# Attention and two fused feed-forward layers on one core: four buffers for raw weight blocks, and a later change of PSUM pools

## The chip, the cores and the metric

The kernel runs on one core of a Trainium2 chip. The metric is device time in microseconds (us) of one launch, as the median of several. A core has a tensor engine (PE, whose weight loads are shown apart as PEld), a vector engine (DVE), a scalar engine (ACT), a general engine (POOL) and a queue for transfers (SP, from which all the transfers named here are issued). PSUM has eight banks; a tile of 128 x 512 f32 fills one.

## The reference

All is f32; in short (softmax, mu and var written as words). The attention result, put back to 2304 tokens of 512, goes through two feed-forward blocks:

```python
scores = scale * np.matmul(q, k.transpose(0, 1, 3, 2))       # 4 x 8 heads, S = 576, D = 64
cum = np.cumsum(np.maximum(s, 0.0), axis=-1)
bias = -(cum[:, :, :, None] - cum[:, :, None, :])
scores = np.where(causal, -1000000000.0, scores + np.minimum(bias, 0.0))
attn = softmax(scores); x = attn @ v
...
a = x @ w1; b = x @ w2                                        # 512 -> 1024
y = (a * b @ w3) @ w_out                                      # 1024 -> 1024 -> 512
...
h = y @ w_in                                                  # 512 -> 1024
solu = h * softmax(h)
ln = (solu - mu) / np.sqrt(var + 1e-06) * g_ln
out = ln @ w_out2                                             # 1024 -> 512
```

## The kernel before, in words

Large products are made of three products of shorter words: each operand is split into a high and a low word by `hi` (a copy with rounding, on ACT) and `lo` (a subtraction, L100, on DVE or POOL), and PE multiplies high by high, high by low and low by high. The Tile framework turns the program into one fixed order of instructions per engine; at run time an engine takes its list from the top and waits at an instruction until the semaphores that it names have come.

**Phase one, the attention (to about 393 us).** A loop of 36 steps. A step does the scores of one head (`sc`; L170 for the first eight heads, L178 and L179 later), its softmax (L192 and L196), and of an earlier head the transposes (`tr`) and the product with V (`av`). Between them lie units of the first feed-forward block: `ab_unit` does 12 matmuls into a tile `a` (L326), which ACT evicts to `a_sb` (L338), and 12 into `b`, which DVE multiplies by `a_sb` into `g_sb` (L346). After the last step 16 such units of the last batch stand alone. For later heads the low words of Q and K (tile QK, L100) are made by POOL.

**Raw weight blocks.** The weights lie in HBM as 64-bit numbers. `stage` (L407) loads a block of 128 x 512 of them, 512 KB, into a buffer named `stage`; `to_f32` turns it into f32 with one pass on ACT (L363) and three on DVE (L369, L370, L374); then `hi` and `lo` make its words, or the f32 block is spilled for later. `load_jobs` keeps as many loads ahead as `stg[1]` says, which is also the number of buffers; in the attention the pool `at` holds two. `pump(n)` converts n blocks; the table PUMP does that in steps 3, 5, 6, 10 to 16 and 22 to 33. After the attention `stg` is set to another pool and four buffers (`mp`), before and after the change.

**Between the phases: M.** M = w3 @ w_out is made in eight blocks f = 0 to 7 by `m_unit`: 24 matmuls of 128 x 512 each (L637), from the words of w3 (`w3h`, `w3l`, eight converted half blocks kept ahead) and of w_out (`WOH`, `WOL`). ACT evicts a block's high word to `MH`, DVE its low word to `ML` (L100). In the same stretch DVE and ACT convert the remaining w3 blocks and make words of spilled weights (`wf_words`: IT..., IB...) and of the first g tile (`split_g`). I call a block's matmuls m0 to m7.

**Phase two.** Per 256 tokens: x = M applied to g (L721, `x2_half`), then h by a seven-product scheme (L753), softmax and layer norm, and the output (L847, `out_unit`). Its PSUM tiles come from psC (four fixed ones) and psD (four turning buffers).

**PSUM pools.** The attention uses psA and psB and from step 11 psE and psF (two fixed banks, six turning). `smalltile` takes the next buffer of the second pool. Where a pool is closed and another opened over its banks, a first write to a bank waits for the last reader of what stood in that bank.

Of the kernel before, what the change touches and what calls it, by code (L numbers as in the profile page):

```python
# [15 lines left out]
PSUM = bass.MemoryType.PSUM  # L16
# [10 lines left out]
def tile_attention_moe(  # L27
# [29 lines left out]
    for i in range(4, 0, -1):  # L57
# [7 lines left out]
    ps_ctx = ExitStack()  # L65
    PSP = [
        ps_ctx.enter_context(tc.tile_pool(name="psA", bufs=2, space=PSUM)),
        ps_ctx.enter_context(tc.tile_pool(name="psB", bufs=4, space=PSUM)),
    ]
# [17 lines left out]
    def smalltile(name):  # L87
        return PSP[1].tile([128, 512], F32, tag="B", name=name)
# [4 lines left out]
    def hi(dst, src, eng=None):  # L93
        if eng is None:
            nc.scalar.activation(out=dst, in_=src, func=AF.Copy)  # L95
        else:
            eng.tensor_copy(out=dst, in_=src)

    def lo(dst, src, hi_, eng=nc.vector):
        eng.tensor_tensor(out=dst, in0=src, in1=hi_.bitcast(F32), op=ALU.subtract)  # L100
# [3 lines left out]
    at = attn_ctx.enter_context(tc.tile_pool(name="at", bufs=1, side="left"))  # L104
# [288 lines left out]
    jobs = []  # L393
    loaded = []

    stg = [at, 2]

    def stage(src):
        raw = stg[0].tile([128, CW, 2], U32, tag="stage", bufs=stg[1], name="stage")
# [15 lines left out]
    def pump(n):  # L415
        for _ in range(n):
            load_jobs()
            if loaded:
                raw, conv = loaded.pop(0)

                with ExitStack() as order:
                    for ins in behind:
                        order.enter_context(tc.issue_after(ins))
                    conv(raw)
        load_jobs()
# [206 lines left out]
    def m_unit(f):  # L632
        ps = smalltile("m")
        for k in range(KF):
            H3, L3 = m_st[f, k // 4]
            for w_, o_ in ((H3, WOH), (H3, WOL), (L3, WOH)):
                nc.tensor.matmul(  # L637
                    ps, w_[:, k % 4], o_[:, k],
                    start=(k == 0 and w_ is H3 and o_ is WOH), stop=(k == KF - 1 and w_ is L3),
                )  # L640
        hi(MH[:, f], ps)
        lo(ML[:, f], ps, MH[:, f])
# [8 lines left out]
    for i in range(8):  # L651
# [7 lines left out]
            nm[0] += 1  # L659
    behind.clear()  # L660
    right0.close()
    ps_ctx.close()
    PSP[:] = [
        ctx.enter_context(tc.tile_pool(name="psC", bufs=1, space=PSUM)),
        ctx.enter_context(tc.tile_pool(name="psD", bufs=4, space=PSUM)),
    ]
    HD = DF // 2

    r2 = ctx.enter_context(tc.tile_pool(name="r2", bufs=1, side="right"))
# [13 lines left out]
    def load_g(c):  # L683
        t0 = c * 256
        g_hl[c] = [None] * KP
        for p in range(KP):
            g_hl[c][p] = [None, r2.tile([128, 2, 256], F32R, tag=f"gl{p}", bufs=2, name=f"gl{p}")]
        for p2_ in range(0, KP, 2):
            done = 0
            while done < 256:  # L690
                n, o = divmod(t0 + done, S)
                w = min(256 - done, S - o)
                for p in (p2_, p2_ + 1):
                    nc.sync.dma_start(
                        out=g_hl[c][p][1][:, :, done:done + w].bitcast(F32),
                        in_=g_scr[n][2 * p:2 * p + 2, :, o:o + w].rearrange("f p t -> p f t"),
                    )
                done += w

    def split_g(c):  # L700
        for p in range(KP):
            raw = g_hl[c][p][1]
            g_hl[c][p][0] = r2.tile([128, 2, 256], F32R, tag=f"gh{p}", bufs=1, name=f"gh{p}")
            hi(g_hl[c][p][0], raw.bitcast(F32))
            lo(raw, raw.bitcast(F32), g_hl[c][p][0], V)
# [190 lines left out]
    def wf_words(i):  # L896
        t = wf.pop(i)
        if i < 14:
            n, j = WN[WL[i]][:-1], int(WN[WL[i]][-1])
            h_, l_ = (x[:, j] for x in IT[n])  # L900
        else:
            h_, l_ = OH[:, i - 14], OL[:, i - 14]
        hi(h_, t)
        lo(l_, t, h_, V)
        wf_load(i + 5)
# [3 lines left out]
        wf_load(i)  # L909
    load_g(1)  # L910
    for f in range(nm[0], KF):
        m_unit(f)
        pump(AM[f])
        if f < 6:
            wf_words(f)
        if f == 5:
            split_g(0)
# [101 lines left out]
```

## Time and profile before

| | |
|---|---|
| three timed runs | 739.62, 737.88, 738.95 us; median 738.95 |
| profiled execution | 737.73 us; span from first to last instruction 736.0 us |
| mean granted PE clock | 0.997 of full speed |
| PE busy | 716.7 us, 97% |
| DVE busy | 504.9 us, 69% |
| ACT busy | 468.0 us, 64% |
| blocks loaded by `stage` | 48 (32 of them counted under `in_w_dram`, 16 under `in_wo_dram`) |

The span is one execution; 1.73 us of its time lie outside the span. Busy shares are means over stages with different limits. Times in rows are from the start of the span.

### The profile page before, as it was taken

What the parts mean: (1) busy time and instruction counts of PE and PEld (TensorE: products, weight loads), DVE (VectorE), ACT (ScalarE), POOL (GpSimd) and SP (SyncE); (2) the same over time, 40 slices, a digit from 0 to 9 for tenths busy, and PEclk for the clock granted to TensorE, in tenths of its full rate; (3) what the DMA queues carried; (4) which work ended last, traced back from release to release, by engine and by line L of the source; (5) the groups of instructions that cost most, each with busy time, mean ns of one, the idle gap of its engine ahead of it and who ended that gap; (6) DMA issues with size and microseconds to landing.
All of it is one profiled execution on the core that took longest, in us unless ns stands there. A gap on an engine that the chain in (4) does not pass through costs nothing.

```text
span 736.0 us, 13040 instructions
## 1 busy us (share of the span) xinstructions
PE 716.7 (97%) x4682; PEld 625.0 (85%) x4682; DVE 504.9 (69%) x1267; ACT 468.0 (64%) x985; POOL 99.5 (14%) x102
## 2 busy tenths in 40 slices
PE   9889998999999999999998999999999999999997
PEld 6567978888888899899997889988888988888886
DVE  7987978897678888632887876576747365563651
ACT  4987777898766777732544745577646465564652
POOL 5033313142221331000000000001000000000000
PEclk9999999999999999999999999999999999999999
DMA  4644554655476665614566943253234142304221
GB/s 109 186 126 99 174 161 142 194 144 130 127 221 186 182 188 149 208 61 147 170 215 202 355 149 101 58 110 75 79 82 101 44 123 75 89 12 75 44 57 44
DMA packets 79829, 95.52 MB, mean 130 GB/s; under 512 B 41418, under 2 KB 52682, under 8 KB 79764
## 3 DMA queue, kind: packets, MB, share of 16 engines
q1 hardware_dynamic: 79764, 94.69, 45.0%
q8 instruction: 37, 0.61, 0.3%
q14 instruction: 28, 0.23, 0.1%
HBM read 59.04 MB, written 20.14 MB: 108 GB/s over the span
## 4 chain that ended last, share of the span: by engine, by line
PE 73%; DVE 11%; DMA 8%; ACT 5%; issue 2%; POOL 1%; SPq 0%; ACTq 0%; DVEq 0%; POOLq 0%
PE x L721 14%; PE o L847 13%; PE b L326 10%; PE a L326 10%; PE hX L753 5%; DMA stage<-in_w_dram 5%; PE av L298 4%; PE hZ L753 3%; PE tr L265 3%; ACT P L196 2%; PE sc L170 2%; PE sc L178 2%; DVE P L192 2%; DVE stage L374 2%; PE hW L753 2%
## 5 line engine op out<-in xcount | busy, mean ns | idle before, releaser
L196 ACT ACTIVATE P<-P,STAT 128x576 f32<-128x576 f32 (+4 forms) x160 | 88.3, 554 | 31.5 <-DVE STAT L192 30.9
L100 POOL TENSOR_TENSOR QK<-qk,QK 64x1152 fp32r<-64x1152 f32 x24 | 67.1, 2798 | 167.2 <-ACT QK L95 158.9
L721 PE MATMUL x<-gl,MH 128*128 128x256 f32 x288 | 80.4, 280 | 0.0
L721 PE MATMUL x<-gh,ML 128*128 128x256 f32 x288 | 80.2, 279 | 0.0
L721 PE MATMUL x<-gh,MH 128*128 128x256 f32 x288 | 79.9, 280 | 0.0
L192 DVE CUSTOM_DVE_ANT_0 P<-sc,wmask 128x576 f32<-128x576 f32 (+4 forms) x160 | 70.6, 478 | 4.5 <-PE sc L170 3.2
L326 PE MATMUL a<-xT0h,W 128*128 128x288 f32 x256 | 58.1, 300 | 1.9 <-ACT a_sb L338 1.9
L326 PE MATMUL b<-xT0h,W 128*128 128x288 f32 x256 | 57.6, 299 | 1.5 <-DVE STAT L192 0.8
L847 PE MATMUL o<-OH,lh 128*128 128x512 f32 x144 | 57.1, 397 | 0.2 <-DVE ll L100 0.2
L326 PE MATMUL a<-xT1h,W 128*128 128x288 f32 x256 | 57.2, 298 | 0.0
L847 PE MATMUL o<-OH,ll 128*128 128x512 f32 x144 | 57.0, 396 | 0.0
L847 PE MATMUL o<-OL,lh 128*128 128x512 f32 x144 | 57.0, 396 | 0.0
L326 PE MATMUL b<-xT1h,W 128*128 128x288 f32 x256 | 56.5, 295 | 0.0
L721 PEld LDWEIGHTS x<-gl,MH 128*128 128x128 f32 x288 | 54.2, 188 | 1.3
L817 DVE COPY lt<-turned 128x2048 uint16<-128x2048 uint16 x16 | 21.9, 1368 | 48.4 <-DMA turned<-half 48.4
L721 PEld LDWEIGHTS x<-gh,MH 128*128 128x128 f32 x288 | 54.0, 188 | 1.1
L721 PEld LDWEIGHTS x<-gh,ML 128*128 128x128 f32 x288 | 54.1, 188 | 0.9
L346 DVE TENSOR_TENSOR g_sb<-b,a_sb 128x288 f32<-128x288 f32 x64 | 28.8, 449 | 32.8 <-PE b L326 16.7
L363 ACT ACTIVATE stage<-stage 128x512 f32<-128x512 f32 x56 | 36.9, 674 | 21.2 <-DMA stage<-in_w_dram 18.0
L298 PE MATMUL av<-PT,VT 128*64 128x64 f32 (+4 forms) x384 | 50.1, 395 | 0.0
L231 ACT ACTIVATE P<-P,STAT 128x576 f32<-128x576 f32 x64 | 42.7, 717 | 10.4 <-DVE STAT L226 10.4
L338 ACT ACTIVATE a_sb<-a 128x288 f32<-128x288 f32 x64 | 25.6, 401 | 33.3 <-PE a L326 33.1
(193 smaller groups left out, 1965.5 us busy)
## 6 DMA issues: line engine op xcount, KB each, us to landing
stage<-in_w_dram SPq DMA_DIRECT2D x32, 512.0 KB
g_scr<-g_sb SPq DMA_DIRECT2D x32, 288.0 KB
stage<-in_wo_dram SPq DMA_DIRECT2D x16, 512.0 KB
qk<-in_qk_dram SPq DMA_DIRECT2D x24, 288.0 KB
QK<-QK SPq DMA_DIRECT2D x24, 288.0 KB
gl<-g_scr SPq DMA_DIRECT2D x24, 256.0 KB
wf<-wf_scr SPq DMA_DIRECT2D x22, 256.0 KB
out_dram<-o SPq DMA_DIRECT2D x18, 256.0 KB
```

The lines of the kernel that those rows point to most:

```text
L100: eng.tensor_tensor(out=dst, in0=src, in1=hi_.bitcast(F32), op=ALU.subtract)
L192: mx = nc.vector.tensor_tensor_reduce(out=dst2, in0=ps_in, in1=msk, scale=-SCALE, scalar=BIG, op0=ALU.add, op1=ALU.min, accum_out=st[0:row ...
L196: ex = nc.scalar.activation(out=dst, in_=dst, func=AF.Exp, bias=st[0:rows, ti:ti + 1], scale=-1.0, accum_out=st[0:rows, 5 + ti:6 + ti],)
L231: nc.scalar.activation(out=dst, in_=dst, func=AF.Copy, scale=r)
L298: nc.tensor.matmul(st["ps"][64 * e:64 * e + 64, 448 + c0:448 + c1], vr[:, j, e], PT[(2 * p + e) % 4][:, o + c0:o + c1], **kw,)
L326: nc.tensor.matmul(ps, w_[:, c, fs], x_[:, c, sl], start=(c == 0 and w_ is WH and x_ is XH), stop=(c == KC - 1 and w_ is WL),)
L338: ab_last[0] = nc.scalar.activation(out=a_sb, in_=ps, func=AF.Copy).ins
L346: ab_last[1] = nc.vector.tensor_tensor(out=g[:, sl], in0=ps, in1=st["a"], op=ALU.mult).ins
L363: nc.scalar.activation(out=high.bitcast(F32), in_=high.bitcast(F32), func=AF.Copy, scale=2.0 ** -112)
L721: last = nc.tensor.matmul(ps[:, a], w_[:, k, m * 128:m * 128 + 128], g_[:, k % 2], start=(k == 0 and w_ is MH and g_ is GH), stop=(k == KF ...
L753: last_h[0] = nc.tensor.matmul(ps, x_[:, k], w_[:, k], start=first and k == 0 and x_ is XH and w_ is WH, stop=k == 1 and x_ is XL, skip_gr ...
L847: nc.tensor.matmul(ps, l_[:, k], w_[:, k], start=(k == 0 and l_ is LH and w_ is OH), stop=(k == KF - 1 and l_ is LL),)
```

## The change

`stage` gets four buffers in the attention, and up to four loads are ahead there. The closing of the attention's pools and the opening of psC and psD move from the end of the attention to the loop over the blocks of M, ahead of block 6: m0 to m5 take tiles of psF, m6 and m7 and everything later tiles of psD.

```diff
--- before.py
+++ after.py
@@ -393,7 +393,7 @@
     jobs = []
     loaded = []
 
-    stg = [at, 2]
+    stg = [at, 4]
 
     def stage(src):
         raw = stg[0].tile([128, CW, 2], U32, tag="stage", bufs=stg[1], name="stage")
@@ -659,11 +659,6 @@
             nm[0] += 1
     behind.clear()
     right0.close()
-    ps_ctx.close()
-    PSP[:] = [
-        ctx.enter_context(tc.tile_pool(name="psC", bufs=1, space=PSUM)),
-        ctx.enter_context(tc.tile_pool(name="psD", bufs=4, space=PSUM)),
-    ]
     HD = DF // 2
 
     r2 = ctx.enter_context(tc.tile_pool(name="r2", bufs=1, side="right"))
@@ -909,6 +904,12 @@
         wf_load(i)
     load_g(1)
     for f in range(nm[0], KF):
+        if f == 6:
+            ps_ctx.close()
+            PSP[:] = [
+                ctx.enter_context(tc.tile_pool(name="psC", bufs=1, space=PSUM)),
+                ctx.enter_context(tc.tile_pool(name="psD", bufs=4, space=PSUM)),
+            ]
         m_unit(f)
         pump(AM[f])
         if f < 6:
```

What the order of instructions shows at three places. Numbers in names count allocated tiles, so the same thing may have another number after the change.

PE, the first block of M. `b_4852` is the last b tile of the attention, `m_4936` (`m_4928` after) is m0. Before:

```order
L326 MATMUL b_4852<-xT1l_132,W12_127 128x288
L326 MATMUL b_4852<-xT1h_131,W13_128 128x288
L637 MATMUL m_4936<-WOH_4263,w3h_4637 128x512 [waits DMAHW3_49,DMAHW4_49,DMAHW2_49,DMAHW6_49,DMAHW1_49,DMAHW7_49,DMAHW0_49,DVE_49]
L637 MATMUL m_4936<-WOL_4264,w3h_4637 128x512
L637 MATMUL m_4936<-WOH_4263,w3l_4638 128x512
```

After:

```order
L326 MATMUL b_4852<-xT1l_132,W12_127 128x288
L326 MATMUL b_4852<-xT1h_131,W13_128 128x288
L637 MATMUL m_4928<-WOH_4263,w3h_4637 128x512 [waits DMAHW5_49,DMAHW4_49,DMAHW6_49,DMAHW3_49,DMAHW7_49,DMAHW0_49,Activation_49]
L637 MATMUL m_4928<-WOL_4264,w3h_4637 128x512
L637 MATMUL m_4928<-WOH_4263,w3l_4638 128x512
```

m0 no longer names a semaphore of DVE; before, that was the last read of `b_4852` (L346), and now there is one of ACT, an eviction of an earlier a tile.

PE, the end of m5 and the start of m6. `m_5183` (`m_5175` after) is m5, `m_5226` is m6. Before:

```order
L637 MATMUL m_5183<-WOL_4264,w3h_5075 128x512
L637 MATMUL m_5183<-WOH_4263,w3l_5076 128x512
L637 MATMUL m_5226<-WOH_4263,w3h_5116 128x512 [waits Activation_49]
L637 MATMUL m_5226<-WOL_4264,w3h_5116 128x512
L637 MATMUL m_5226<-WOH_4263,w3l_5117 128x512 [waits DVE_49]
```

After:

```order
L637 MATMUL m_5175<-WOL_4264,w3h_5067 128x512
L637 MATMUL m_5175<-WOH_4263,w3l_5068 128x512
L637 MATMUL m_5226<-WOH_4263,w3h_5108 128x512 [waits DVE_49]
L637 MATMUL m_5226<-WOL_4264,w3h_5108 128x512
L637 MATMUL m_5226<-WOH_4263,w3l_5109 128x512
```

The first matmul of m6 waited for the words of w3 on ACT; it now waits for DVE, by the count the low word ML of m5, which stands in the same bank as m6 does now.

PE, further on in m6. `m_5253` is m7, `x2_5286` the first tile of phase two. Before:

```order
L637 MATMUL m_5226<-WOH_4263,w3h_5124 128x512 [waits Activation_49]
L637 MATMUL m_5226<-WOL_4264,w3h_5124 128x512
L637 MATMUL m_5253<-WOH_4263,w3h_5163 128x512 [waits Activation_49]
L637 MATMUL m_5253<-WOL_4264,w3h_5163 128x512
L721 MATMUL x2_5286<-gh0_5214,MH_4258 128x256 [waits DMAHW4_49,DMAHW3_49,DMAHW5_49,DMAHW2_49,DMAHW6_49,DMAHW1_49,DMAHW7_49,DMAHW0_49,DVE_49]
L721 MATMUL x2_5286<-gl0_4910,MH_4258 128x256
L721 MATMUL x2_5286<-gh0_5214,ML_4259 128x256
```

After:

```order
L637 MATMUL m_5226<-WOH_4263,w3h_5116 128x512 [waits Activation_49]
L637 MATMUL m_5226<-WOL_4264,w3h_5116 128x512
L637 MATMUL m_5253<-WOH_4263,w3h_5155 128x512 [waits Activation_49]
L637 MATMUL m_5253<-WOL_4264,w3h_5155 128x512
L716 MATMUL x2_5286<-gh0_5206,MH_4258 128x256 [waits DMAHW4_49,DMAHW5_49,DMAHW3_49,DMAHW6_49,DMAHW2_49,DMAHW7_49,DMAHW1_49,DMAHW0_49]
L716 MATMUL x2_5286<-gl0_4902,MH_4258 128x256
L716 MATMUL x2_5286<-gh0_5206,ML_4259 128x256
L637 MATMUL m_5226<-WOH_4263,w3l_5117 128x512 [waits DVE_49]
```

Before, 20 matmuls of x stand here before m6 goes on; now three, and 12 more matmuls of m6 and m7 come earlier than those of x. Up to here m6 has done 12 matmuls in both.

DVE, around the low word of m2 (`m_5038` before, `m_5030` after); the L369 with `stage_4971` (`stage_4963`) is the first pass of a raw w3 block that waits for its load. Before:

```order
L100 TENSOR_TENSOR IB21l_4892<-wf_4926,IB21h_4891 128x512 [waits DMAHW4_49,Activation_49]
L100 TENSOR_TENSOR w3l_5025<-stage_4875,w3h_5024 128x512 [waits PE_49,Activation_49]
L369 TENSOR_SCALAR stage_4971<-stage_4971 128x512 [waits DMAHW1_49]
L370 SCALAR_TENSOR_TENSOR stage_4971<-stage_4971 128x512 [waits DVE_49,Activation_49]
L100 TENSOR_TENSOR ML_4259<-m_5038,MH_4258 128x512 [waits Activation_49]
```

After:

```order
L100 TENSOR_TENSOR IB21l_4884<-wf_4918,IB21h_4883 128x512 [waits DMAHW4_49,Activation_49]
L100 TENSOR_TENSOR w3l_5017<-stage_4875,w3h_5016 128x512 [waits PE_49,Activation_49]
L100 TENSOR_TENSOR ML_4259<-m_5030,MH_4258 128x512 [waits Activation_49]
L369 TENSOR_SCALAR stage_4963<-stage_4963 128x512 [waits DMAHW1_49]
L370 SCALAR_TENSOR_TENSOR stage_4963<-stage_4963 128x512 [waits DVE_49,Activation_49]
```

ML of m2 now stands ahead of the two passes of that block. Between this place and ML of m5 both orders hold the same passes but for this one.

## Rows read from the trace of the kernel before

**Rows 1.** The page's busy time by engine, over the whole span.

```profile
PE 716.7 (97%) x4682; PEld 625.0 (85%) x4682; DVE 504.9 (69%) x1267; ACT 468.0 (64%) x985; POOL 99.5 (14%) x102
```

**Rows 2.** Busy time, clock, DMA share and GB/s in three windows of the attention.

```profile
73.00:160.00 87.00, 81.71 (x623) 73.28 (x622) 76.02 (x221) 70.90 (x177) 23.28 (x8) 1.00 0.56 166
160.00:300.00 140.00, 140.00 (x1104) 125.52 (x1102) 108.67 (x323) 107.07 (x272) 35.87 (x13) 1.00 0.60 171
300.00:320.00 20.00, 18.80 (x149) 18.24 (x146) 12.95 (x40) 12.41 (x30) 0.00 (x0) 1.00 0.46 150
```

**Rows 3.** Waits from 73 to 160 us: total, times, longest.

```profile
DVE stage L369 <- DMA stage<-in_w_dram: 10.0, 8, 3.1
...
ACT stage L363 <- DMA stage<-in_w_dram: 4.1, 3, 2.8
```

**Rows 4.** The chain from 73 to 165 us, by line.

```profile
by line: DMA stage<-in_w_dram 23.6%; DVE P L192 11.3%; DVE W L100 10.5%; DVE stage L374 7.2%; DVE stage L370 6.1%; DVE P L233 5.8%; PE b L326 5.7%; PE a L326 5.5%; DVE PT L97 4.7%; issue 3.6%; ACT P L196 2.0%; PE tr L265 1.9%; PE sc L178 1.
```

**Rows 5.** Timeline of ACT: four evictions of an a block.

```profile
74.55 0.41 ACT L338 ACTIVATE a_sb<-a 128x288 f32<-128x288 f32 x1 [0.60 <-PE a L326]
...
160.01 0.39 ACT L338 ACTIVATE a_sb<-a 128x288 f32<-128x288 f32 x1
...
198.80 0.39 ACT L338 ACTIVATE a_sb<-a 128x288 f32<-128x288 f32 x1
...
220.90 0.39 ACT L338 ACTIVATE a_sb<-a 128x288 f32<-128x288 f32 x1
```

**Rows 6.** The chain from 296 to 322 us: start, length, what.

```profile
303.68 6.18 DMA stage<-in_wo_dram
...
309.93 0.68 ACT stage L363
...
314.54 1.58 PE a L326 x12
```

**Rows 7.** Lo passes of tile W (ns minimum/median/maximum); two spans, POOL and DVE.

```profile
L100 DVE TENSOR_TENSOR W<-stage,W x16: 643/677/2461, 29.0 to 155.0; 128x512 fp32r<-128x512 f32 x16
...
82.74 5.76 POOL L100 TENSOR_TENSOR QK<-qk,QK 64x1152 fp32r<-64x1152 f32 x2 [13.42 <-ACT QK L95]
...
86.59 2.46 DVE L100 TENSOR_TENSOR W<-stage,W 128x512 fp32r<-128x512 f32 x1
```

**Rows 8.** Timeline where the blocks of M begin.

```profile
393.38 0.29 PE L326 MATMUL b<-xT1h,W 128*128 128x288 f32 x1
...
395.21 0.45 DVE L346 TENSOR_TENSOR g_sb<-b,a_sb 128x288 f32<-128x288 f32 x1
...
395.72 0.50 PE L637 MATMUL m<-WOH,w3h 128*128 128x512 f32 x1 [2.05 <-DVE g_sb L346]
```

**Rows 9.** Windows of the blocks of M and behind them, columns as above.

```profile
396.50:400.00 3.50, 3.50 (x10) 2.71 (x9) 3.04 (x6) 2.41 (x4) 0.00 (x0) 0.51 0.37 114
412.00:416.00 4.00, 4.00 (x19) 3.34 (x18) 1.55 (x3) 0.62 (x2) 0.00 (x0) 1.00 1.03 399
420.00:432.00 12.00, 12.00 (x55) 9.94 (x54) 12.00 (x23) 8.91 (x16) 0.00 (x0) 1.00 0.82 255
444.00:600.00 156.00, 156.00 (x951) 138.98 (x950) 98.48 (x202) 96.94 (x149) 11.24 (x16) 1.00 0.35 87
```

**Rows 10.** Timeline of DVE at 415 and of both engines at 433.

```profile
415.32 0.43 DVE L369 TENSOR_SCALAR stage<-stage 128x512 uint32<-128x512 uint32 x1 [2.20 <-DMA stage<-in_w_dram]
...
433.05 0.39 PE L637 MATMUL m<-WOL,w3h 128*128 128x512 f32 x1
...
433.43 0.69 DVE L100 TENSOR_TENSOR ML<-m,MH 128x512 fp32r<-128x512 f32 x1
...
433.68 0.50 PE L637 MATMUL m<-WOH,w3h 128*128 128x512 f32 x1 [0.24 <-ACT w3h L95]
...
434.02 0.40 PE L637 MATMUL m<-WOL,w3h 128*128 128x512 f32 x1
...
434.26 0.28 PE L721 MATMUL x<-gh,MH 128*128 128x256 f32 x1
```

## Prediction

> **What bounds the kernel now.** I read the page's busy times first: PE is busy 716.7 us of a span of 736.0 [rows 1], so all that a change can win back at PE without taking away work is some twenty microseconds, and the question is in which stretches PE loses them. Windows of busy time, moved along the span, answer that: PE is solid from 160 to 300 us, 140.00 of 140 [rows 2], and from 444 to 600, 156.00 of 156 [rows 9]. It loses in three places that the change touches: 5.3 us between 73 and 160 us, 1.2 us between 300 and 320 [rows 2], and 2.05 us where the blocks of M begin [rows 8].
>
> In the first place the waits say who is late: DVE waits 10.0 us and ACT 4.1 us for loads of raw weight blocks [rows 3], and the chain of that stretch, which is 92 us long, lies on such loads for 23.6%, that is 21.7 us [rows 4]. The reader should see that these are waits of DVE, not of PE; PE waits for DVE and ACT one step later. In the second place the chain is one load of 6.18 us, a conversion pass on ACT, and then PE's next a block [rows 6]: ACT couldn't evict a block while it stood at the conversion. In the third place PE waits for the last read of a b tile by DVE, `g_sb`, and afterwards runs at a granted clock of 0.51, the lower of the two levels, from 396.5 to 400 [rows 8, 9].
>
> Idle time alone misses stretched work, so I took the pace as well. Two a evictions 22.1 us apart, at 198.80 and 220.90 [rows 5], enclose two heads and four units; four units are 96 matmuls of 1.58/12 = 0.132 us [rows 6], 12.7 us, which leaves 4.7 us for a head. Between the evictions at 74.55 and 160.01 the written order has 302 matmuls of units (39.8 us) and parts of heads that amount to about 7.4 (34.8 us): about 75 us at the steady pace, against 85.5 taken. The loss of the first place is thus between 5.3 us (idle shown) and 10.5 us (pace). The early heads have other score matmuls, so the 75 is an estimate.
>
> **Part one, four buffers.** It removes no instruction; loads are issued up to four ahead. Between steps 10 and 16 there are 13 blocks, and four of them can now lie ready, so I cost the DVE and ACT waits [rows 3] at nothing afterwards. They don't turn into PE time one for one: from 73 to 160 DVE is busy 76.0 us of 87 [rows 2], as much as PE's 75, and each engine's order is fixed, so both would have to run without a gap to win everything. Bounds are 1.2 us (two bad meetings, below) and 10.5 us (all of the loss). I take about half of the larger, 4.8: DVE would then be busy 76.0 of 82.2 us, 92%. For the second place I take its 1.2 us whole; a load issued two conversions earlier covers one of 6.18 us [rows 6], bounds 0 and 1.2. Sum of part one: -6.0 us.
>
> The added transfers are the same ones earlier. SP issues four loads where it issued two at first, and later ones ahead of some copies of QK words. The DMA share between 73 and 160 is 0.56 [rows 2], so I cost that at nothing; the room in the queues is the cover. If a QK copy came late, the next head's scores would wait, up to one load's 6.18 us [rows 6] in a bad case.
>
> **Part two, the pools.** At the beginning of M, m0 now names only an eviction on ACT that lies several blocks back. It can follow the last b matmul, which starts at 393.38 [rows 8]. That saves 2.05 us, and if the clock stays up also 3.5 x 0.49 = 1.7 us [rows 9]: the blocks m0 to m5 would end 3.75 us earlier.
>
> This gain ends at m6. There DVE sets the time: it is busy 12.00 of 12 us from 420 to 432 [rows 9], after a stretch in which the loads pace it (DMA share 1.03, DVE only 1.55 of 4 us, from 412 to 416 [rows 9]; one pass waits 2.20 us for a load [rows 10]). ML of m5 starts at 433.43 and ends at 434.12 [rows 10], long after m5's matmuls. Neither bound depends on when PE starts M. The one thing that moves is ML of m2, which now stands ahead of the pass that waited 2.20 us: it falls into that idle time, and all behind it is up to one pass, 0.6 us, earlier. So ML of m5 ends at about 433.5.
>
> Before, m6 asked for nothing but its weights and PE went on: its 14 matmuls and two of m7 were done when x started at 434.26 [rows 10]. At 12.00/55 = 0.218 us a matmul [rows 9], and with the first of m7 due at 433.05 + 0.22, m6 began at 433.27 - 14 x 0.218 = 430.2. Now PE is done with m5 at 430.2 - 3.75 = 426.4 and stands at m6's first matmul until 433.5, 7.1 us, for behind it on PE's list stand 16 matmuls of m6 and m7 and then x, and none may pass. Those 16 take 3.5 us, so x starts at 437.0 in place of 434.26: +2.8. The idle of 7.1 us is longer than the 2.05 that came before the low clock of M's start; I price the same again, +1.7. Sum +4.5. What was won at the start of M is worth nothing, since the same DVE pass is waited for in the end. Nothing later takes it up, because PE is solid behind it [rows 9]. Bounds: 0 (clock stays up and ML comes 2.8 us sooner) and 2.8 + 2 x 1.7 = 6.2. The order also brings 12 matmuls of m6 and m7 ahead of x; the same work, but they wait for w3 words that x used to cover, which I leave inside the bound.
>
> **Sum.** -6.0 + 4.5 = -1.5 us on the profiled execution's 737.73, which gives 736.2. That execution lies 1.22 us below the median of 738.95, so on the median's scale 737.5.
>
> **The rivals.**
>
> *Slower: DVE keeps the time in the attention.* Some low-word passes of W on DVE take 2.46 us where the median is 0.68: the one at 86.59 lies under two POOL passes on Q and K that run from 82.74 to 88.50 [rows 7]. Each such meeting costs 1.8 us. Conversions that no longer wait for their load move, and two more of them may land under the eight POOL passes of this stretch [rows 2]: 3.6 us of the 4.8 are gone, and DVE, as loaded as PE, hands them on. Then -1.2 - 1.2 + 4.5 = +2.1, 741.0. It decides from one such meeting on, where the sum is +0.3. Speaking for it: these passes are 10.5% of the chain [rows 4]. Against: the waits that go may equally free passes from meetings.
>
> The Trainium skill, GPSIMD Engine Reference, section 1, states that POOL's SBUF interfaces are shared with VectorE, with contention for DVE instructions that have two SBUF inputs. The low-word pass is one, and the trace agrees with 2.46 us against 0.68 [rows 7]. By this rule as a cost of every conversion that meets POOL the sum would be the 741.0 of this rival; by the median row it is 737.5.
>
> *Much faster: the loads were all that held the attention.* Then all of the 10.5 us comes back: -10.5 - 1.2 + 4.5 = -7.2, 731.8. For it: the chain's 21.7 us on loads [rows 4]. Against: DVE would be busy 76.0 of 76.5 us.
>
> *M costs almost nothing.* If the clock doesn't fall after the wait at m6 and ML of m5 is 1.3 us sooner still, because w3 loads are less in each other's way, +1.5 stays: 734.5. Against: DVE's solid 12 us have no gap to close.
>
> *The low clock lasts twice as long.* The wait at m6 is over three times the one at M's start; another 1.7 us gives +0.2, 739.2.
>
> That the new orders don't do what the edits say can be left out for m0 and m6, since their waits are written in the order. For the buffers it would mean loads that are late with any number of buffers; a share of 0.56 speaks against it.
>
> **How the numbers follow.** My forecast, within 2 us of 737.5, gets 0.50; the slower rival 0.22; the much faster one 0.14; the cheap M 0.09; the long low clock 0.05. A change of 0.2%, 1.5 us, is about what can be told from none. Half of the forecast's chance lies below 737.5; with the faster two that is 0.25 + 0.14 + 0.09 = 0.48 for faster. Its other half and most of the long low clock make 0.29 for the same. The rest, 0.23, is slower. The forecast's own range is 735.5 to 739.5. For 8 in 10 it has to reach to the middle of the much faster case and about to that of the slower one: 732.5 to 741.5, which leaves out half of each, 0.07 and 0.11.
>
> **What would show it.** If part one is right, the waits of DVE and ACT for loads between 73 and 160 us fall from 14 us to under 3, and the a eviction that stood at 160.01 comes 3 to 7 us sooner. Longer W passes in their place, or a chain that goes from DVE to DVE, would speak for the slower rival; an eviction at 150 for the much faster. If part two is right, m0 starts within 0.3 us of the last b matmul's turn at full clock, a wait of some 7 us for ML of m5 stands at m6's first matmul, and the clock falls behind it. From the a eviction near 220 us to the first x matmul the time should be longer than before by about 3 us, leaving out the 1.2 of the second place. The prediction is wrong if ML of m5 follows PE (it would come some 3 us sooner with m5), or if the attention gives less than 3 or more than 8 us.

## Result and the profile after

The change is slower: 746.88 us, median of 5 (746.06 to 749.21), against 738.68 of the kernel before in the same series; the ratio is 1.0115, 95% interval 1.0097 to 1.0132. The forecast was 737.5, between 732.5 and 741.5. The profiled execution took 746.06 us, its span 744.3, 8.3 more than before.

Busy time by engine, from the page, the line that answers to [rows 1]:

```profile
PE 719.7 (97%) x4682; PEld 628.2 (84%) x4682; DVE 508.9 (68%) x1267; ACT 467.6 (63%) x985; POOL 98.4 (13%) x102
```

PE is busy 3.0 us longer with the same 4682 matmuls, and idle 5.3 us longer. Where, the windows tell (columns as in [rows 2]; compare with [rows 2, 9]):

```profile
73.00:160.00 87.00, 79.07 (x569) 71.16 (x569) 75.34 (x202) 66.22 (x162) 21.54 (x8) 0.94 0.53 156
92.00:100.00 8.00, 7.05 (x32) 7.05 (x33) 7.03 (x24) 5.67 (x12) 0.00 (x0) 0.57 0.52 171
132.00:137.00 5.00, 4.04 (x18) 3.88 (x19) 5.00 (x13) 3.94 (x10) 0.00 (x0) 0.66 0.31 85
160.00:300.00 140.00, 140.00 (x1107) 126.58 (x1104) 109.57 (x327) 107.48 (x273) 36.66 (x14) 1.00 0.57 164
300.00:320.00 20.00, 20.00 (x161) 18.02 (x160) 15.79 (x51) 15.62 (x42) 0.00 (x0) 1.00 0.47 154
434.00:440.00 6.00, 2.81 (x7) 2.23 (x8) 5.26 (x10) 2.87 (x5) 0.00 (x0) 0.50 0.39 124
444.00:600.00 156.00, 156.00 (x960) 139.40 (x959) 92.94 (x190) 91.23 (x142) 9.54 (x14) 1.00 0.32 80
```

From 73 to 160 us the granted clock is 0.94 where it was 1.00, PE's idle time 7.9 us where it was 5.3, and about 50 matmuls less were done. Two stretches hold the low clock, at 92 and at 132. From 300 to 320 PE is now solid. In M, between 434 and 440, it runs at 0.50. From 444 to 600 it is solid again, as before.

Four evictions of an a block on ACT, which answer to [rows 5], and the last one:

```profile
74.55 0.41 ACT L338 ACTIVATE a_sb<-a 128x288 f32<-128x288 f32 x1 [0.59 <-PE a L326]
...
164.80 0.41 ACT L338 ACTIVATE a_sb<-a 128x288 f32<-128x288 f32 x1
...
205.08 0.39 ACT L338 ACTIVATE a_sb<-a 128x288 f32<-128x288 f32 x1
...
227.19 0.38 ACT L338 ACTIVATE a_sb<-a 128x288 f32<-128x288 f32 x1
...
397.30 0.38 ACT L338 ACTIVATE a_sb<-a 128x288 f32<-128x288 f32 x1
```

The first stands where it stood. The one at 160.01 is 4.8 us later, those at 198.80 and 220.90 are 6.3 us later; the last one came at 392.63 before and is 4.7 later. The first x matmul starts at 442.49 (434.26 in [rows 10]), 8.2 later. So the span splits into +6.3 us between the first and the 21st eviction, -1.6 up to the last, +3.6 from there to the first x, and +0.1 behind.

The waits from 73 to 160 us, in which lines for raw weight blocks stood before [rows 3]:

```profile
PE b L326 <- DVE g_sb L346: 5.4, 2, 2.8
...
PE b L326 <- DVE STAT L192: 1.5, 1, 1.5
```

No wait for a load of a raw block is left there, of 14 us; PE waits for a DVE eviction instead. The timeline shows how such a wait comes about:

```profile
84.43 5.74 POOL L100 TENSOR_TENSOR QK<-qk,QK 64x1152 fp32r<-64x1152 f32 x2 [15.10 <-ACT QK L95]
...
84.95 2.71 DVE L370 SCALAR_TENSOR_TENSOR stage<-stage 128x512 uint32<-128x512 uint32 x1
...
88.27 2.45 DVE L370 SCALAR_TENSOR_TENSOR stage<-stage 128x512 uint32<-128x512 uint32 x1
...
91.24 1.28 DVE L374 SCALAR_TENSOR_TENSOR stage<-stage 128x512 uint32<-128x512 uint32 x2
...
92.45 0.45 DVE L346 TENSOR_TENSOR g_sb<-b,a_sb 128x288 f32<-128x288 f32 x1
...
92.95 0.61 PE L326 MATMUL b<-xT0h,W 128*128 128x288 f32 x1 [2.55 <-DVE g_sb L346]
...
127.00 3.17 DVE L374 SCALAR_TENSOR_TENSOR stage<-stage 128x512 uint32<-128x512 uint32 x1
...
132.96 0.37 PE L326 MATMUL b<-xT0h,W 128*128 128x288 f32 x1 [2.81 <-DVE g_sb L346]
```

POOL's two passes on Q and K end at 90.17. Under them two conversion passes of DVE take 2.71 and 2.45 us. Behind those stand a low-word pass and two more conversions, and only then `g_sb` at 92.45, which sets a PSUM buffer free; PE had to wait 2.55 us for it, and its clock was low about from then on. The same happens at 127 to 133, with one pass of 3.17 us. The same place before the change, behind the pass of 2.46 us in [rows 7]:

```profile
79.10 0.46 DVE L346 TENSOR_TENSOR g_sb<-b,a_sb 128x288 f32<-128x288 f32 x1
...
88.97 0.44 DVE L346 TENSOR_TENSOR g_sb<-b,a_sb 128x288 f32<-128x288 f32 x1
...
89.47 0.40 PE L326 MATMUL b<-xT0h,W 128*128 128x288 f32 x1 [0.65 <-DVE g_sb L346]
```

There DVE needed 9.87 us from the third `g_sb` to the fourth and PE waited 0.65 us; with the change it is 12.48 us, from 79.97 to 92.45.

M, the answer to [rows 8, 10]:

```profile
398.40 0.39 PE L637 MATMUL m<-WOH,w3h 128*128 128x512 f32 x1
...
436.45 0.68 DVE L100 TENSOR_TENSOR ML<-m,MH 128x512 fp32r<-128x512 f32 x1
...
437.19 0.79 PE L637 MATMUL m<-WOH,w3h 128*128 128x512 f32 x1 [5.99 <-DVE ML L100]
...
442.49 0.28 PE L716 MATMUL x<-gh,MH 128*128 128x256 f32 x1
```

m0 follows the last b matmul without a wait. m6 waits 5.99 us for the low word of m5, as forecast, and runs on at the lower clock.

### The profile page after: what moved, and what is told of

It is laid out like the page before. It is cut to its first block, busy times and chain, and to the rows that moved or that the text cites. A ratio compares the mean times of both kernels' runs of the same rounds, so it can differ in the third digit from the quotient of the medians.

```text
span 744.3 us, 13033 instructions
## 1 busy us (share of the span) xinstructions
PE 719.7 (97%) x4682; PEld 628.2 (84%) x4682; DVE 508.9 (68%) x1267; ACT 467.6 (63%) x985; POOL 98.4 (13%) x102
## 4 chain that ended last, share of the span: by engine, by line
PE 84%; DVE 7%; ACT 3%; DMA 2%; issue 2%; POOL 1%; SPq 0%; ACTq 0%; DVEq 0%; POOLq 0%
PE x L716 14%; PE o L842 13%; PE b L326 13%; PE a L326 13%; PE av L298 6%; PE hX L748 5%; PE tr L265 4%; PE hZ L748 3%; PE sc L178 2%; PE sc L179 2%; PE sc L170 2%; PE m L637 2%; PE hW L748 2%; PE hY L748 2%; DVE stage L374 2%
## 5 line engine op out<-in xcount | busy, mean ns | idle before, releaser
L326 PE MATMUL a<-xT0h,W 128*128 128x288 f32 x256 | 59.6, 305 | 0.0
L346 DVE TENSOR_TENSOR g_sb<-b,a_sb 128x288 f32<-128x288 f32 x64 | 28.9, 451 | 39.0 <-PE b L326 23.0
L326 PEld LDWEIGHTS b<-xT0h,W 128*128 128x128 f32 x256 | 43.9, 192 | 8.0 <-ACT PT L95 3.0
```

The costliest lines, as they stand in the source:

```text
L326: nc.tensor.matmul(ps, w_[:, c, fs], x_[:, c, sl], start=(c == 0 and w_ is WH and x_ is XH), stop=(c == KC - 1 and w_ is WL),)
L346: ab_last[1] = nc.vector.tensor_tensor(out=g[:, sl], in0=ps, in1=st["a"], op=ALU.mult).ins
```

## Experiments

Each was timed against the kernel before on the same chip in the same series. Ratios are of time to that of the kernel before, with their 95% intervals. The three lengths are from one profile each: from the first to the 21st a eviction, from there to the 64th, and from there to the first x matmul (starts on ACT and PE). The first eviction starts between 73.91 and 79.21 us in these profiles; the lengths leave that difference out.

A profile is one execution, and not always a typical one: run 9's is 3.5 us slower than its median, run 10's 3.9 us faster. How far the lengths can be trusted is seen where the attention's order is the same: before, 2, 5 and 9 have 124.25, 124.25, 126.21 and 124.96 in the first stretch. In all four PE waits 1.6 us at the same `sc` matmul. Before and in run 2 the clock stays up behind it, in runs 5 and 9 it falls, as here before the change and then in run 5:

```profile
123.76 0.37 PE L178 MATMUL sc<-QK 128*128 128x288 f32 x1 [1.60 <-issue]
...
123.00:128.00 5.00, 3.57 (x23) 3.10 (x24) 5.00 (x13) 4.97 (x15) 3.59 (x1) 1.00 0.44 118
```

```profile
126.14 0.37 PE L178 MATMUL sc<-QK 128*128 128x288 f32 x1 [1.60 <-issue]
...
126.00:131.00 5.00, 4.18 (x19) 3.98 (x20) 5.00 (x14) 4.51 (x15) 3.56 (x1) 0.66 0.44 118
```

So a difference of less than 2 us between two first stretches says little.

| kernel | median us | ratio | 1st to 21st | 21st to 64th | 64th to x |
|---|---|---|---|---|---|
| before | 738.68 | 1 | 124.25 | 193.83 | 41.63 |
| changed | 746.88 | 1.0115 (1.0097 to 1.0132) | 130.53 | 192.22 | 45.19 |
| 1 four buffers alone | 742.62 | 1.0050 (1.0028 to 1.0072) | 130.53 | 191.99 | 40.75 |
| 2 pools alone | 743.79 | 1.0071 (1.0033 to 1.0109) | 124.25 | 193.72 | 46.47 |
| 3 four buffers, short POOL | 735.90 | 0.9967 (0.9944 to 0.9990) | 123.98 | 192.52 | 41.12 |
| 4 before, short POOL | 738.91 | 1.0002 (0.9972 to 1.0031) | 124.84 | 192.84 | 40.58 |
| 5 pools changed behind M | 741.77 | 1.0016 (0.9990 to 1.0041) | 126.21 | 193.36 | 50.48 |
| 6 the same, late buffers | 740.95 | 1.0000 (0.9981 to 1.0020) | 124.74 | 192.32 | 52.04 |
| 7 four buffers, words on DVE | 738.27 | 0.9962 (0.9945 to 0.9979) | 126.37 | 192.12 | 40.62 |
| 8 three buffers alone | 737.84 | 0.9967 (0.9946 to 0.9988) | 125.97 | 191.96 | 40.39 |
| 9 pools changed at m7 | 742.89 | 1.0045 (1.0022 to 1.0069) | 124.96 | 193.69 | 52.28 |
| 10 before, words on DVE | 736.96 | 0.9962 (0.9941 to 0.9983) | 121.65 | 191.97 | 40.66 |
| 11 three buffers, words on DVE | 736.96 | 0.9965 (0.9945 to 0.9985) | 124.45 | 192.10 | 41.65 |
| 12 changed, words on DVE | 743.01 | 1.0045 (1.0024 to 1.0065) | 126.37 | 192.40 | 46.03 |

The median of before was 738.91 us in the series of runs 1 to 4, 740.40 in 5 to 8, 739.18 in 9 to 11 and 739.60 in 12. In runs 5, 6 and 9 the first x stands behind all matmuls of M, so their last column is not to be compared with the others.

**The theories.** After the result I held: the conversions, which no longer wait for loads, stand closer together and in other places of DVE's list, some of their passes fall under POOL's passes ahead of an eviction, PE waits for that and comes back at the lower clock; and apart from that, the wait at m6. Rivals: DVE's new order alone costs, whatever POOL does; or the pools' edit reaches into the attention.

**1 and 2. Each edit alone.**

```diff
-    stg = [at, 2]
+    stg = [at, 4]
```

> Four buffers alone, the pools as before. Matching a evictions of the changed kernel and the one before puts +6.3 us between 74 and 165 us, -1.4 us around 300 us and +3.6 us in the blocks of M. If the two edits add up, this kernel keeps the first two: +4.9 us, about 743.6, with the waits for raw blocks gone and two stretches at the lower clock between 88 and 140 us. If the attention's loss came from the pools too (another order of its last part), it would be within 1 us of before.

```diff
     for f in range(nm[0], KF):
+        if f == 6:
+            ps_ctx.close()
+            PSP[:] = [ ... ]
```

The lines at the end of the attention go, as in the change; so they do in runs 5 and 6.

> The pools' edit alone, two buffers. If the edits add up: a wait of about 6 us for the low word of m5 at m6's first matmul, the lower clock behind it, +3.5 us, about 742.2, and the attention as before. If the pools cost nothing with an undisturbed attention in front: no change or 2 us faster.

Measured 0.50% and 0.71% more, together 1.21%, where the change has 1.15%: the edits add up. The first stretch is 130.53 us with four buffers and 124.25 with the pools' edit, exactly as in the changed kernel and in the one before. So the attention's loss is that of the buffers, and the rival that the pools cause it falls. With the pools alone the wait at m6 is:

```profile
434.44 0.80 PE L637 MATMUL m<-WOH,w3h 128*128 128x512 f32 x1 [7.00 <-DVE ML L100]
```

and the window behind it shows the lower clock:

```profile
432.00:437.00 5.00, 2.56 (x6) 2.08 (x7) 4.26 (x8) 2.17 (x4) 0.00 (x0) 0.50 0.35 109
```

The forecast for this wait was 7.1 us.

**3 and 4. POOL's passes cut short.** The low words of Q and K are made for 8 of 576 columns and are zero elsewhere; that part of the computation is left out.

```diff
-        lo(t[64:128, 1::2], raw, t[64:128, 0::2], G)
+        lo(t[64:128, 1::2, 0:8], raw[:, :, 0:8], t[64:128, 0::2, 0:8], G)
...
                 aug_rows(t[:, 0], t[:, 3])
+                nc.gpsimd.memset(t[64:128, 1::2].bitcast(F32), 0.0)
```

> As the four buffers alone, but POOL makes the low words of Q and K for only 8 of 576 columns, the others are zero (set once): that part of the computation is left out, so that POOL hardly touches SBUF while DVE converts. To be compared with the same cut in the kernel before. If passes of DVE stretched by POOL (2.45 to 3.17 us in place of 0.68) make PE wait and drop its clock, the attention's loss goes, and this one is 3 to 8 us faster than the cut kernel with two buffers. If the new order of DVE, with conversion passes gathered ahead of evictions, is enough by itself, it stays 4 to 6 us slower than that one.

> The kernel before with the same part left out (low words of Q and K beyond 8 columns are zero). If stretched passes matter: up to 4 us faster than before, the four stretched passes between 84 and 150 us back at 0.7 us each, while the 10 us of waits for raw blocks stay. If they are hidden: no change.

With POOL's passes cut short four buffers gain 0.33% instead of losing 0.50%, and the first stretch falls from 130.53 to 123.98 us. The kernel with two buffers does not move, within 0.3% either way. The window of run 3 and then of run 4:

```profile
73.00:160.00 87.00, 82.70 (x623) 74.49 (x622) 66.95 (x221) 71.46 (x181) 5.49 (x8) 0.98 0.57 169
```

```profile
73.00:160.00 87.00, 81.70 (x613) 73.70 (x613) 68.34 (x223) 71.64 (x175) 3.47 (x8) 0.98 0.58 170
```

DVE is busy 67 us in place of 75, and no conversion pass is longer than 0.8 us. The order of run 3's DVE list has the same numbers of conversion passes between evictions as that of the changed kernel, so this order does no harm by itself. But the first stretch is also just 0.9 us shorter than in run 4, with one spell of the lower clock in each: in these profiles the loads' waits were worth hardly anything to PE. The medians lie 3.0 us apart, at the low end of what was expected; of the two profiles' difference 2.2 us stand ahead of the first eviction, where profiles differ anyway, so the waits may be worth somewhat more than 0.9.

**5 and 6. The pools changed behind all of M; and four buffers only late.**

```diff
     for f in range(nm[0], KF):
         m_unit(f)
         ...
+    ps_ctx.close()
+    PSP[:] = [ ... ]
     mctx.close()
```

> Two buffers; the attention's pools stay open for all eight blocks of M and are changed behind the last one, so that no block of M takes a bank whose low word is still to be read. If that shared bank is the cause of the 6 us wait at m6: no such wait, no low clock in M, m0 without its 2.05 us, and a time 1 to 2.5 us under before (3.75 us won at the start of M, about 1.3 lost at the end, where the last words of w3 pace PE and no matmul of x stands in between). If keeping the pools open costs by itself, it is 3 to 5 us slower, as the pools' edit alone was.

Run 6 adds to that:

```diff
+    turn_s = [0, 0]
     def stage(src):
-        raw = stg[0].tile([128, CW, 2], U32, tag="stage", bufs=stg[1], name="stage")
+        turn_s[0] ^= turn_s[1]
+        tag, n = ("stage", stg[1]) if stg[0] is not at else ("stage" + "B" * turn_s[0], 2)
+        raw = stg[0].tile([128, CW, 2], U32, tag=tag, bufs=n, name="stage")
...
-        while jobs and len(loaded) < stg[1]:
+        while jobs and len(loaded) < stg[1] + 2 * turn_s[1]:
...
+        if st == 18:
+            turn_s[1] = 1
```

> As the run before, and four buffers only from step 18 on (two names of two buffers each; up to then two). DVE's order up to the 33rd eviction is that of before. If the loss in the attention belongs to the conversions of steps 10 to 16 and the gain around 300 us to the later blocks: 1.2 to 1.4 us faster than the run before. If the attention's stretched passes come back somewhere else: no faster, or slower.

Both came out at no change. The wait at m6 for a low word is gone, so that part holds, but the gain was priced wrong, and the clock does fall in M. PE's waits in run 5 between 390 and 450 us, the longest and the one at x, and the window of the first:

```profile
PE m L637 <- ACT w3h L95: 2.5, 1, 2.5
PE x L716 <- DVE ML L100: 1.4, 1, 1.4
...
433.00:438.00 5.00, 4.08 (x10) 2.66 (x11) 4.26 (x8) 1.78 (x3) 0.00 (x0) 0.66 0.39 107
```

Without x matmuls between them the last blocks of M wait for words of w3, and the first x waits for the low word of m7: the change of pools finds its price in the new place. In run 6 the second stretch is 1.0 us shorter than in run 5, but the two timings do not tell the runs apart.

**7. Four buffers, low words on DVE.** Nothing is left out.

```diff
-        lo(t[64:128, 1::2], raw, t[64:128, 0::2], G)
+        lo(t[64:128, 1::2], raw, t[64:128, 0::2], V)
```

> Four buffers alone, with all the low words of Q and K made by DVE in place of POOL, nothing left out. DVE gets 8 more passes between 73 and 160 us, some 1.5 us each by the width (1152 columns against 512 in 0.68 us). If passes stretched by POOL are what costs, and not DVE's order or load: no pass over 0.8 us, and 2 to 6 us faster than four buffers alone, 737 to 741. If DVE's load or order costs: as slow as four buffers alone or slower, 743 or more.

738.27 us, 0.38% under before; beside four buffers alone that is nearly 0.9% less, as the first theory had it. Its first stretch, though, is 126.37, longer than in run 3. One wait stands out in it:

```profile
98.70 0.52 PE L265 MATMUL tr<-ident,P 128*128 128x128 f32 x3 [2.00 <-DVE P L233]
```

```profile
98.00:103.00 5.00, 4.30 (x21) 3.45 (x22) 4.94 (x16) 4.95 (x13) 0.00 (x0) 0.63 0.66 194
```

PE waits 2.00 us for DVE, and the clock is down behind it. Passes of 1.35 us in DVE's list take the place of the stretched ones; that they cause this wait was not tried apart.

**8. Three buffers alone.**

```diff
-    stg = [at, 2]
+    stg = [at, 3]
```

> Three buffers alone, pools as before. By the order, seven conversion passes stand between the third and fourth eviction of a unit, where two buffers have five and four buffers nine. If the number of passes gathered ahead of an eviction decides: halfway, 1.5 to 2.5 us slower than before. If it is where passes fall under POOL's: the loss goes with the number and length of passes over 1.5 us between 73 and 160 us (four before, 4.6 us too long; four with four buffers, 8.3 us), and may be nothing.

0.33% faster. Three passes with two inputs are stretched (2.45, 2.46 and 2.15 us, together 5.0 too long, as against 5.3 before and 8.3 with four buffers; the 4.6 of the expectation was summed wrongly). No wait of PE is longer than 1.63 us. The halfway loss of the other theory did not come. But the sum of stretching doesn't decide either: passes with one input are stretched too, and with all that take over 1.5 us the excess is 9.3 us before, 11.9 here and 12.4 with four buffers. What differs is how long DVE takes from one `g_sb` to the next: from the third to the fourth 9.87 us before, 11.09 here and 12.48 with four buffers, from the ninth to the tenth 7.80, 6.96 and 10.85.

**9. The pools changed at m7.** The edit is that of run 2 with `f == 7`.

> Two buffers, the pools changed ahead of block 7 in place of 6. m7's tile stands in bank 4, where m2 stood, whose low word is long read; m6 stands in bank 6. If a bank's own last reader is what is waited for, m7 doesn't wait for a low word at all, and the time is within 1 us of before or up to 3 faster. If the change of pools waits for the last reader of any tile of the old pools, m7's first matmul waits for the low word of m6, made just ahead of it, with the lower clock behind, and the kernel is 2 to 5 us slower than before, like the change at m6.

0.45% slower, and m7 waits for the low word of m6:

```profile
443.84 0.69 DVE L100 TENSOR_TENSOR ML<-m,MH 128x512 fp32r<-128x512 f32 x1 [2.72 <-ACT MH L95]
...
444.58 0.50 PE L637 MATMUL m<-WOH,w3h 128*128 128x512 f32 x1 [1.41 <-DVE ML L100]
```

m7's bank was long free, by the order. So a change of pools waits for the last reader of any tile of the old pools, not for that of one bank. Run 2 says the same: in its order m5 stands in bank 3 and m6 in bank 4, and m6 waits for the low word of m5 all the same. In the profile this wait is not the largest, though. PE's other waits there are for words of w3, and the clock has fallen ahead of m7, not behind it as expected:

```profile
PE m L637 <- DVE w3l L100: 2.2, 1, 2.2
PE m L637 <- ACT w3h L95: 1.2, 1, 1.2
...
436.00:444.00 8.00, 5.01 (x12) 3.13 (x10) 4.54 (x9) 1.93 (x3) 0.00 (x0) 0.57 0.25 66
```

**10, 11 and 12. Low words on DVE with two buffers, with three, and with the whole change.** The edit is that of run 7, put on the kernel before, on run 8's and on the changed one.

> Two buffers, the low words of Q and K made by DVE, nothing else changed. Together with four buffers this gave 0.38% less time than before. If POOL's meetings cost only where loads no longer wait, this is within 1.5 us of before (with POOL's passes cut to 8 columns the kernel before stayed at 1.0002). If DVE's additional 1.35 us passes cost, it is 1 to 3 us slower.

> Three buffers and the low words of Q and K on DVE. Three buffers alone were 0.33% faster than before, four with the words on DVE 0.38%. If both gains come from the same source (blocks that no longer wait, and no stretched pass ahead of an eviction), they do not add: 736 to 739, 2 to 3.5 us faster than before. If they are separate, about 5 us faster.

> The whole change, with the low words of Q and K made by DVE in place of POOL. If the change's loss is the sum of stretched passes in the attention and of the wait at m6, only the second stays: four buffers with the words on DVE were 0.38% faster than before (-2.8 us), the pools alone 0.71% slower (+5.2) by their own run and +3.6 us by the trace of the change; together +0.8 to +2.5 us, 740 to 741.7, some 6 us faster than the change itself. If the attention's loss has another source that only shows with both edits: 744 or more.

Run 10 was a miss: two buffers with the words on DVE are 0.38% faster, neither the same nor slower. From 73 to 160 us its profile has the clock at 1.00 and 2.65 us of idle PE:

```profile
73.00:160.00 87.00, 84.35 (x641) 75.27 (x640) 78.45 (x231) 73.00 (x183) 0.00 (x0) 1.00 0.58 169
```

Run 11 is no faster than runs 8 and 10, so the gains don't add. Run 12 lies 0.45% over before, 0.7% under the change; its first stretch is that of run 7 to the hundredth, and m6 waits as in the change:

```profile
PE m L637 <- DVE ML L100: 6.2, 1, 6.2
```

It lies between the two forecasts for it: M's part stays, the attention's part falls by 4.2 of 6.3 us and not to nothing.

## Why the prediction was wrong

**The step that failed** is the term of part one, "about half of the larger, 4.8": the attention did not gain 4.8 us, it lost 6.3. Three things were wrong in it.

*The waits for loads were taken for time of PE.* All of them went, as forecast (14 us to none), and PE got little for them: even with POOL's passes cut short, four buffers are 0.9 us better than two in that stretch (profiles of runs 3 and 4; 3.0 us in the medians of the whole). The chain's 21.7 us on loads [rows 4] led to DVE's passes, most of which had slack towards PE. The estimate of 75 us at the steady pace, which set the upper bound, was never approached: the shortest first stretch of any run, run 10's, is 2.6 us under before.

*The buffers were taken to leave DVE's list as it was.* They don't: with more buffers the written order has the passes earlier and in larger groups. Between the third and the fourth `g_sb`, where PE waits 2.55 us, stand nine conversion passes where five stood; ahead of the tenth, where it waits 2.81 us, stand six where five stood (counted in the orders, low-word passes of W included). I read this order for M and not for the attention. Every pass in front of a `g_sb` can hold up PE, whose next matmul in the order needs the buffer that `g_sb` frees.

*The price of a meeting with POOL was too low, and the clock was left out of it.* The slower rival named the mechanism, and at two additional meetings of 1.8 us gave 741.0. In fact no meeting was added: there are four stretched passes with two inputs before and after, and two of over 1.5 us with one input. But the four are longer (2.45, 2.70, 2.71 and 3.17 us, where before had 1.79, 1.85, 1.96 and 2.46, the last in [rows 7]), all four are conversions where three were low-word passes, and more work stands between them and the next eviction. At the fourth `g_sb` DVE takes 2.6 us more than before, of which stretching is only 0.7; the rest comes from the four passes more. At the tenth it takes 3.05 us more, and there the pass of 3.17 us makes 2.5 of it. Before, the longest PE wait for an eviction behind them was 0.66 us; now there are two of 2.55 and 2.81. Each goes with the lower clock: 0.06 of 87 us, 5.2 us, is the larger part of the loss, and 2.6 us more idle time (over the same matmuls) the smaller. The two together are 7.8, more than the 6.3 lost; in 0.66 us of the low clock PE stood idle anyway, and the rest of the difference was not traced. The prediction priced the clock only in M.

Neither part does it alone. Stretched passes in the order of before cost nothing that could be measured (run 4 equals before within 0.3%), the order of four buffers without them costs nothing (run 3). With POOL's words made by DVE the profiles have four buffers 4.7 us longer in the first stretch than two (runs 7 and 10), and a 1.35 us pass ahead of a gathered group may work like a stretched one, if less; but the timings put both runs at 0.9962, so a loss there is not shown. The Trainium skill, GPSIMD Engine Reference, section 1, names the contention of POOL and DVE at SBUF for DVE instructions with two SBUF inputs; the trace agrees, L370 and L374 included, with up to 3.17 us against 0.68. Passes with one tensor input were stretched as well (an L369 of 2.03 us before, against 0.42).

**The later blocks** were right: -1.2 forecast, -1.6 measured, and PE is solid from 300 to 320.

**M** was right in its mechanism and near in its size: +4.5 forecast, +3.6 in the changed kernel and +4.8 with the pools alone. m0 starts without a wait (-2.0 from the last a eviction on), m6 waits 5.99 and 7.00 us (7.1 forecast) for a low word of m5 that ends 5.4 us ahead of the first x in the changed kernel, and the lower clock lasts beyond it, in the changed kernel for 3.3 us, which is a loss of 1.6 where the prediction took 1.7. The change's shorter wait has its low word at 437.13, which is 1.7 us sooner than before once the 4.7 us of delay are taken off, 1.1 more than forecast. One reason given ahead of the prediction is wrong though: that m6 and m5 share bank 4 is a coincidence; the wait is for the whole old pool (runs 2 and 9). That is why no place for the change of pools was free: at the end of the attention it costs the 2.05 us of [rows 8] and a spell of low clock, at m6 a wait of 6 to 7 us, behind M what run 5 shows.

**The range** ended at 741.5 because the slower rival was priced without the clock; with the 5.2 us of the clock its sum would have been +7.3, 746.3. That this is near the 746.88 measured is in part luck: that rival still has 1.2 us of gain in the attention ahead of the clock, where 1.1 us were lost, and M came 0.9 us cheaper than its 4.5.

## What to carry to other kernels

A wait that the chain blames on a transfer belongs to the engine that waits; ask first whether the bounding engine waits for that engine, and read in the written order what a transfer that comes earlier will push ahead of the instruction that frees the bounding engine's buffers. Where such an instruction stands behind a group of passes, price the lower clock together with the wait, since here it was twice as dear (5.2 us against 2.6). A change of PSUM pools waited, wherever it was put here, for the last reader of all the old tiles: put it where the engines that empty PSUM are least behind, not where PE would like it.

## What was unexpected in the hardware

A meeting of DVE and POOL has a simple form in these rows. Each of the eight stretched passes with two inputs, four before and four after, ends 0.55 us behind the POOL pass under which it began: at 89.05 behind 88.50 before [rows 7], at 90.72 behind 90.17 with the change. So it costs what is left of POOL's pass when DVE's begins, up to 2.5 us here, and not a fixed 1.8. The reverse occurs too: before the change a conversion that began shortly after a POOL pass (at 124.19) ran at its usual 0.67 us, and that POOL pass took 3.59 us, where the median of the 24 is 2.68.

Low words of Q and K on DVE take 1.35 us where POOL took 2.7, and with two buffers this one edit makes the kernel 0.38% faster than before, better than both kernels (736.96 us, interval of the ratio 0.9941 to 0.9983). Handing these passes to POOL was no help here.

The lower clock went with PE waits of 2.00 us (run 7), 2.55, 2.81 and 5.99 us (changed kernel). The length of the wait alone does not decide it: the same wait of 1.6 us in the same order was followed by 1.00 before and in run 2 and by the lower level in runs 5 and 9, and one of 1.69 us at m0 in run 10 by 1.00. What does decide was not tested.

What stays open: that run 8 keeps its PE waits short because DVE takes less time between evictions was read from its profile and not tried apart; why run 10 is faster than before where run 4 is not (their intervals overlap); and whether a DVE list with the evictions written ahead of the conversions would let four buffers gain was not tried.
